# Two attention-fed MLPs on one core: raw weights read in pairs, and the order of the first batch rebuilt

## The chip, the cores and the metric

The kernel runs on one core of one Trainium2 chip. Its time is device microseconds of one launch. Three runs of the kernel before took 931.21, 931.71 and 933.12 us; the median is 931.71 us.

## The reference, cut to what matters

Windowed and global attention over 4 batches and 8 heads, then a gated MLP on normed rows, then a second MLP; everything is float32 in and out.

```python
batch, n_heads, seq_l, seq_g, head_dim = (4, 8, 512, 32, 64)
s_g  = scale * q_g @ k_all.T;   out_g = softmax(s_g) @ v_all        # 32 global queries see everything
s_ll = where(|i - j| <= 32, scale * q_l @ k_l.T, -1e9)              # 512 local queries: a window
s_l  = concat([scale * q_l @ k_g.T, s_ll]);  out_l = softmax(s_l) @ concat([v_g, v_l])
x = concat([out_g, out_l]).transpose(0, 2, 1, 3).reshape(B * S, H * D)   # 4 * 544 = 2176 rows
xn = x / sqrt(mean(x * x) + 1e-6) * rms_g                           # rms_g: 512 gains
y = (silu(xn @ w_gate) * (xn @ w_val)) @ w_out                      # w_gate, w_val: 512 x 1536, w_out: 1536 x 512
h = y @ w_in;  out = maximum(0.01 * h, h) @ w_out2                  # 512 x 2048, 2048 x 512
```

The weights come to the device as 64-bit words (512 KB for a 128 x 512 block) and are narrowed to float32 there.

## The kernel before, in words

**Attention** goes by half units `k` (two query tiles of 128 of one head pair; `half_unit`, L242). A half unit has the steps p (products into PSUM), e (masked maximum on VectorE L263, exp on ScalarE L266), n (norm on VectorE, L278 to L286), t (transposes on TensorE, L302 and L304), c and d (copies of the transposed weights, on ScalarE and VectorE, L311), v (values on TensorE, into `po`) and x (copy of the result to `xl`, L338). The global queries of a head pair are a `global_pair` (L350): G1 scores and their maximum, Gn norm, G2 turned weights, G3 values (`pz_g`), G4 the copies of the result into `x_glob` (L422, L423). `vz` holds the values of the global keys, brought by DMAs that GpSimd issues (L236); `bd` holds the global queries of a batch, block-diagonal.

**The first batch** is written by hand: the string `FIRST` (L484) is read item by item and each item issues its instructions, so every engine gets its own in that order. q, s and g are the first block's norm: squares (L552), their sums (L563) and the multiplication by the gains (`xg`, L570, with the gains in `gcol`); R is the root; a and o narrow one block of weights (`a01`: step 0, block 1); L loads a part of a later unit and Q loads global queries.

**The first MLP** takes its 2176 rows in three blocks of 512 and a tail of 640 in two halves. A block has 12 steps f of 128 hidden columns. A step has three weight blocks k: 0 gate, 1 value, 2 out. In block 0 they come as raw words (`w_0`, `w_1`, ... in the trace, tags w640, w641, w642 with 2, 2 and 1 buffers) by `fetch` (L710), are narrowed by `convert` (L739: one ScalarE instruction `nc` L108, two VectorE instructions `nr` L110 and `wf` L115), stored as float32, split into a high and a low part (`halves_of`, L89 and L92) and multiplied as three products (`mm3`, L85). Steps 0 and 1 use the float32 weights directly (L1005). Block 1 reads the float32 weights back, stores the split form and the sums that the tail needs (`sums_of`); block 2 reads the split form. Beside blocks 0 to 2 the attention of batches 1 to 3 runs, at places given by the table `PLAN`. In block 2 the gaps also take the second MLP's weights (`raw2`, `narrowed`, L874 to L915): 32 jobs of 512 KB, each one load (`w64b`), one narrowing and one store, each load one job ahead.

The first batch, the tail and the second MLP run in the order of the code. Between them the framework's scheduler sets the order of each engine from the code and the pins (`PINS`). A buffer of a pool is filled again only when its last reader is done, and a queue (SP's above all) works in order: a load that waits for a buffer holds up all that stands behind it.

## Time and profile before

| | us |
|---|---|
| runs | 931.21, 931.71, 933.12 (median 931.71) |
| profiled execution | 927.5 |
| its span in the trace | 925.7 |
| TensorE busy in the span | 903.1 (98%) |
| VectorE, ScalarE, GpSimd busy | 616.3, 464.1, 54.4 |
| DMA traffic | 218.05 MB, 236 GB/s on average |

The span runs from the first to the last instruction of the trace; the profiled execution is 1.8 us longer. TensorE is idle for 925.7 - 903.1 = 22.6 us in the span. Timelines have one row for each run of like instructions; a bracket at its end gives the idle time of that engine just before it and what ended it. Where a wait is for several things, the one that came last by the profile is named.

### The profile page before, as it was taken

The numbers are of one execution on the slowest core, as the hardware profiler recorded it, in microseconds if no ns is written. First come the engines' busy times: TensorE is split into PE (matmuls) and PEld (weight loads), VectorE is DVE, ScalarE is ACT, GpSimd is POOL, SyncE is SP. The second block draws the span as 40 slices with busy tenths as digits, with TensorE's granted clock in tenths as the row PEclk, the third lists the DMA queues.
The fourth block names the chain that finished last, engine by engine and source line by source line (L and its number), as shares of the span: only waits on it lengthen the run. The fifth ranks groups of instructions, "written<-read, shape, count | busy, mean of one in ns | idle before, by whom it ended". The sixth has DMA issues, their size and how long they took to land.

```text
span 925.7 us, 14767 instructions
## 1 busy us (share of the span) xinstructions
PE 903.1 (98%) x5172; PEld 737.3 (80%) x5172; DVE 616.3 (67%) x1376; ACT 464.1 (50%) x985; POOL 54.4 (6%) x130
## 2 busy tenths in 40 slices
PE   6889999999999999999999999999999999999998
PEld 5547777777777777877899999888888888888886
DVE  6799977697767886764787776777566344454332
ACT  6977765555554554545634443555544233344321
POOL 6300010100101000000000000000000000000000
PEclk9999999999999999999999999999999999999999
DMA  9898995898889999974477586776433286631122
GB/s 243 275 357 303 311 339 183 265 337 282 296 289 372 373 414 397 347 244 142 151 280 256 185 277 202 265 262 228 148 93 110 72 300 220 215 127 58 46 62 98
DMA packets 91307, 218.05 MB, mean 236 GB/s; under 512 B 13280, under 2 KB 28640, under 8 KB 89184
## 3 DMA queue, kind: packets, MB, share of 16 engines
q1 hardware_dynamic: 88160, 216.05, 67.7%
q0 software_dynamic: 3072, 1.05, 0.5%
q8 instruction: 41, 0.67, 0.3%
q14 instruction: 34, 0.28, 0.1%
HBM read 150.47 MB, written 66.58 MB: 234 GB/s over the span
## 4 chain that ended last, share of the span: by engine, by line
PE 86%; DMA 4%; DVE 2%; ACT 1%; SPq 1%; issue 0%; DVEq 0%
PE o L85 19%; PE pg L85 10%; PE yp L85 10%; PE pv L85 9%; PE px L85 5%; PE pz L85 4%; PE py L85 4%; PE yt L85 4%; PE po L156 3%; PE sc L156 3%; PE pw L85 2%; PE tz L85 2%; PE tx L85 2%; PE ty L85 2%; DMA w64b<-w 2%; PE po L85 1%
## 5 line engine op out<-in xcount | busy, mean ns | idle before, releaser
L85 PE MATMUL o<-wr,d 128*128 128x512 f32 x768 | 174.4, 389 | 0.0
L85 PEld LDWEIGHTS o<-wr,d 128*128 128x128 f32 x768 | 144.1, 188 | 29.9
L85 PE MATMUL pg<-xh,w 128*128 128x512 f32 x272 | 88.9, 408 | 1.0 <-ACT xh L89 1.0
L85 PE MATMUL pv<-xh,w 128*128 128x512 f32 x272 | 86.5, 399 | 0.0
L85 PE MATMUL yp<-hsh,w 128*128 128x512 f32 x288 | 84.8, 399 | 0.9 <-ACT hsh L89 0.9
L266 ACT ACTIVATE s_ring<-s_ring,mx 128x224 f32<-128x224 f32 x128 | 60.6, 478 | 33.2 <-DVE mx L263 33.1
L85 PEld LDWEIGHTS yp<-hsh,w 128*128 128x128 f32 x288 | 53.2, 188 | 14.1 <-issue 1.9
L92 DVE TENSOR_TENSOR d<-h,d 128x512 fp32r<-128x512 f32 x64 | 42.0, 688 | 33.4 <-ACT d L89 33.4
L85 PEld LDWEIGHTS pg<-xh,w 128*128 128x128 f32 x272 | 48.5, 188 | 17.0 <-issue 4.9
L85 PEld LDWEIGHTS pv<-xh,w 128*128 128x128 f32 x272 | 49.6, 188 | 11.6 <-issue 0.5
L89 ACT CAST d<-h 128x512 fp32r<-128x512 f32 x64 | 38.3, 621 | 35.9 <-PE o L85 35.9
L85 PE MATMUL pg<-xl,w 128*128 128x512 f32 x136 | 53.7, 395 | 0.0
L85 PE MATMUL pv<-xl,w 128*128 128x512 f32 x136 | 53.3, 392 | 0.0
L89 ACT CAST w<-wf 128x512 fp32r<-128x512 f32 x68 | 41.5, 618 | 19.9 <-PE pv L85 16.3
L85 PE MATMUL pz<-ysb,wr 128*128 128x512 f32 x192 | 49.1, 391 | 0.0
L85 PE MATMUL yp<-hsl,w 128*128 128x512 f32 x144 | 49.1, 398 | 0.0
L263 DVE CUSTOM_DVE_ANT_0 s_ring<-sc,masks 128x224 f32<-128x224 f32 x128 | 42.9, 389 | 8.5 <-POOL vz L1067 4.9
L236 POOL DMA_DIRECT2D vz<-v_b x64 | 32.0, 503 | 257.5 <-PE po L156 253.5
L92 DVE TENSOR_TENSOR w<-wf,w 128x512 fp32r<-128x512 f32 x68 | 46.4, 689 | 0.7 <-ACT w L89 0.7
L92 DVE TENSOR_TENSOR wr<-wr 128x1024 fp32r<-128x1024 f32 x16 | 19.6, 1225 | 40.3 <-ACT wr L89 40.2
L1302 ACT ACTIVATE h<-h 128x1536 f32<-128x1536 f32 x16 | 23.8, 1490 | 42.8 <-DVE h L954 42.8
L85 PE MATMUL yt<-hst,w 128*128 128x320 f32 x288 | 42.6, 309 | 0.8 <-DMA w<-w_dram 0.8
(227 smaller groups left out, 1790.9 us busy)
## 6 DMA issues: line engine op xcount, KB each, us to landing
w<-w_dram SPq DMA_DIRECT2D x72, 512.0 KB, 5.1
w<-w SPq DMA_DIRECT2D x36, 512.0 KB, 6.3
w_dram<-w SPq DMA_DIRECT2D x36, 512.0 KB, 4.8
w64b<-w SPq DMA_DIRECT2D x32, 512.0 KB, 7.7
w_dram<-wr SPq DMA_DIRECT2D x8, 1792.0 KB, 8.1
wr<-w_dram SPq DMA_DIRECT2D x8, 1792.0 KB, 7.4
kq<-kqv SPq DMA_DIRECT2D x32, 352.0 KB, 6.1
w_f<-wf SPq DMA_DIRECT2D x36, 256.0 KB, 5.2
```

What stands on the lines that cost most here:

```text
L85: nc.tensor.matmul(dst, lhs[a], rhs[b], start=first and i == 0, stop=last and i == 2, skip_group_check=onto)
L89: nc.scalar.copy(hi, src)
L92: nc.vector.tensor_tensor(out=lo, in0=src, in1=hi.bitcast(F32), op=ALU.subtract)
L156: x = nc.tensor.matmul(dst, lhs, rhs, start=start, stop=stop, skip_group_check=bool(onto))
L236: queue.dma_start(out=vz_ring[u % 3][r:r + SG, i, c], in_=v_b[b, p][0:SG, 0, c])
L263: nc.vector.tensor_tensor_reduce(out=sp, in0=sc[j][:, i * KW:(i + 1) * KW], in1=mask_of(t), scale=-scale, scalar=3.0e38, op0=ALU.add, op1= ...
L266: x = nc.scalar.activation(out=sp, in_=sp, func=AF.Exp, bias=mx[:, c:c + 1], scale=-1.0, accum_out=sm[:, c:c + 1])
L1302: nc.scalar.activation(out=out, in_=x, func=AF.Prelu, alpha=0.01)
```

## The change

1. **Gate and value weights of a step go as one.** The raw words of both are one transfer of 1 MB into one tile (tag w64, 2 buffers); they are narrowed one after the other at the place of the value weights; the float32 form is one store and one read of 512 KB (`w_both`). The out weight keeps its own (w642, 1 buffer; `w_last`). The sums for the tail use w642's one buffer in place of w640's two, and are read back as one. Float32 tiles: 2 of double size (wfb) and 3 single (wf), in place of 7 single.
2. **The second MLP's raw weights** come as 16 jobs of 1 MB into the same w64 tiles, in place of 32 jobs of 512 KB.
3. **The first batch is rebuilt.** Masks and `vz` are cleared by VectorE; GpSimd makes the first masks, then `ident`, then issues the first `vz` loads, then makes the last mask. The products of half unit 0 go to four PSUM banks in place of two. The first batch's global queries come by one DMA, and two GpSimd copies put them into `bd`. The gains come as 4 rows of 128 and are turned by TensorE (item c) in place of a DMA of 512 single elements. G01 is cut in G0p (products) and G0e (maximum, exp) with n2 between; `FIRST` has a new order; E0, the load of the exp table, is an item of its own in place of standing right behind the root; a02 and o02 (the out weight of step 0) are now in `FIRST`.

```diff
-            wraw[g, k] = mb.tile([P, DM, 2], U32, tag=f"w64{k}", bufs=W64[k], name=f"w64{k}_{f}")
-            nc.sync.dma_start(out=wraw[g, k], in_=words(w1[f])[:, k])
+            if k:
+                t = mb.tile([P, DM, 2], U32, tag="w642", bufs=1, name=f"w642_{f}")
+                wraw[g, 2] = t
+                nc.sync.dma_start(out=t, in_=words(w1[f])[:, 2])
+            else:
+                t = mb.tile([P, 2, DM, 2], U32, tag="w64", bufs=2, name=f"w64_{f}")
+                wraw[g, 0], wraw[g, 1] = t[:, 0], t[:, 1]
+                wraw[g, "both"] = t.rearrange("p k c t -> p (k c) t")
+                nc.sync.dma_start(out=t, in_=words(w1[f])[:, 0:2])
...
+    def full_tile(g, k):
+        if k:
+            wf[g, 2] = mp.tile([P, DM], F32, tag="wf", bufs=3, name=f"wf2_{g}")
+            return
+        t = wf[g, "both"] = mp.tile([P, 2 * DM], F32, tag="wfb", bufs=2, name=f"wfb_{g}")
+        wf[g, 0], wf[g, 1] = t[:, 0:DM], t[:, DM:2 * DM]
...
+        if k == 0:
+            return
+        full_tile(g, k - 1 if k == 1 else k)
...
+            if k == 1:
+                for x in range(2):
+                    narrow(mb, wf[g, x], wraw[g, x], f"{x}_{f}")
+            else:
+                narrow(mb, wf[g, 2], wraw[g, 2], f"{k}_{f}")
         kept_weights(g, k)
...
-        nc.sync.dma_start(out=w1_f32[step_of(g)[1]][k], in_=wf[g, k])
+        if k == 1:
+            nc.sync.dma_start(out=w1_both[f].rearrange("p k c -> p (k c)"), in_=wf[g, "both"])
+        else:
+            nc.sync.dma_start(out=w1_last[f], in_=wf[g, 2])
         if step_of(g + W64[k])[0] == 0:
-            fetch(g + W64[k], k)
+            fetch(g + W64[k], k - 1 if k == 1 else k)
...
-        ws = mb.tile([P, 4, HK], F32, tag="w640", bufs=W64[0], name=f"ws{f}")
+        ws = mb.tile([P, 4, HK], F32, tag="w642", bufs=1, name=f"ws{f}")
...
-    def narrowed(f, k):
+    def narrowed(f):
         raws = []
         def make():
-            wf = mp.tile([P, DM], F32, tag="wf", bufs=7, name=f"wfb{k}_{f}")
-            narrow(mb, wf, raws[0], f"b{k}_{f}")
-            nc.sync.dma_start(out=w2_f32[f][k], in_=wf)
-        return [lambda: raws.append(raw2(f, k)), make]
+            t = mp.tile([P, 2 * DM], F32, tag="wfb", bufs=2, name=f"wfc_{f}")
+            for k in range(2):
+                narrow(mb, t[:, k * DM:(k + 1) * DM], raws[0][:, k * DM:(k + 1) * DM], f"c{k}_{f}")
+                nc.sync.dma_start(out=w2_f32[f][k], in_=t[:, k * DM:(k + 1) * DM])
+        return [lambda: raws.append(raw2(f)), make]
...
+            qs = qg_t[:, b * NP:(b + 1) * NP, :]
+            if not b:
+                t = mb.tile([P, P], F32, tag="rs", name=f"qs{b}").rearrange("p (n q) -> p n q", q=SG)
+                nc.sync.dma_start(out=t, in_=qs)
+                qs = t
...
+                    nc.gpsimd.tensor_copy(bd[0][r, :, o:o + SG], qs[r])
...
     FIRST = ("p0 e0 p1 e1 "
-             "n0 p2 t0 c0 e2 d0 Q0 "
-             "n1 p3 v0 t1 c1 x0 e3 d1 G01 "
-             "n2 p4 v1 t2 c2 x1 z0 e4 d2 q0 s0 g0 L40 L41 L50 L51 "
+             "n0 p2 t0 c0 e2 d0 "
+             "n1 p3 v0 t1 c1 x0 e3 d1 G0p "
+             "n2 G0e p4 v1 t2 c2 x1 z0 e4 d2 c L40 L41 L50 L51 "
              "n3 p5 v2 t3 c3 x2 e5 d3 G0n G02 "
-             "n4 p6 v3 t4 c4 x3 e6 d4 a00 "
-             "n5 p7 v4 t5 c5 x4 e7 d5 o00 G03 r0 L42 "
-             "n6 v5 t6 c6 x5 q1 g1 n7 d6 G04 t7 "
-             "s1 v6 c7 x6 q2 d7 L52 "
-             "v7 s2 x7 q3 s3 g2 R0 g3 a01 o01 a10 a11 o10 o11")
+             "n4 p6 v3 t4 c4 x3 e6 d4 a00 q0 "
+             "n5 p7 v4 t5 c5 x4 G03 e7 d5 o00 s0 r0 L42 "
+             "n6 v5 t6 n7 c6 d6 t7 v6 c7 x5 d7 q1 v7 s1 x6 q2 s2 x7 L52 Q0 "
+             "q3 s3 g0 R0 g1 a01 g2 o01 g3 a02 a10 o02 E0 a11 o10 G04 o11")
...
-            nc.scalar.activation(out=early_root, in_=eps, func=AF.Exp)
             anchors["recip"] = nc.vector.reciprocal(out=rs[:, 0:m], in_=rs[:, 0:m]).ins
...
-        with nc.allow_non_contiguous_dma(reason="512 gains, one column a chunk"):
-            nc.sync.dma_start(out=gcol, in_=rms_g.rearrange("(c p) -> p c", p=P))
+        nc.sync.dma_start(out=grow, in_=rms_g.rearrange("(c p) -> c p", p=P))
```

How it moves the instructions, at three places. First GpSimd at the start of the kernel: `masks` are the window masks, `bd` the global queries, `vz` the global values that `po` needs. Before:

```order
L188 AFFINE_SELECT masks<-masks 128x32
L191 MEMSET masks 128x32
L196 MEMSET bd_197 64x4x32
L197 MEMSET bd_197 64x4x32
L196 MEMSET bd_198 64x4x32
L197 MEMSET bd_198 64x4x32
L1067 MEMSET vz_190 128x256
L236 DMA vz_190<-v_b 32x64 x4
L1067 MEMSET vz_191 128x256
L236 DMA vz_191<-v_b 32x64 x4
```

After:

```order
L193 AFFINE_SELECT masks<-masks 128x32
L196 AFFINE_SELECT masks<-masks 128x32
masks.py:197 MEMSET ident 128x128
masks.py:199 AFFINE_SELECT ident<-ident 128x128
L244 DMA vz_178<-v_b 32x64 x4
L186 AFFINE_SELECT masks<-masks 128x128
L188 AFFINE_SELECT masks<-masks 128x128
L193 AFFINE_SELECT masks<-masks 128x32
L244 DMA vz_179<-v_b 32x64 x4
L244 DMA vz_180<-v_b 32x64 x4
```

The first four `vz` loads now stand ahead of the last mask and of all of `bd`.

Second ScalarE at the end of the first batch: `pt` are transposed attention weights, `po` attention results on their way to `xl`, `sq` squares of the first block's norm, `xg` the rows times their gains. Before:

```order
L552 ACTIVATE sq_1_721<-xl_409 128x512
L570 ACTIVATE xg<-xl_409,gcol 128x512
L422 COPY x_glob<-px_g_732 64x2x32
L423 COPY x_glob<-px_g_732 64x2x32
L311 COPY pt_7_757<-pp_7_736 128x512
L338 COPY xl_409<-po_744 128x256
L552 ACTIVATE sq_2_760<-xl_409 128x512
L338 COPY xl_409<-po_772 128x256
L552 ACTIVATE sq_3_787<-xl_409 128x512
L570 ACTIVATE xg<-xl_409,gcol 128x512
L594 ACTIVATE rs<-pm_790,eps 128x128
```

After:

```order
L320 COPY pt_6_710<-pp_6_697 128x512
L320 COPY pt_7_734<-pp_7_714 128x512
L347 COPY xl_397<-po_684 128x256
L583 ACTIVATE sq_1_739<-xl_397 128x512
L347 COPY xl_397<-po_721 128x256
L583 ACTIVATE sq_2_756<-xl_397 128x512
L347 COPY xl_397<-po_741 128x256
L583 ACTIVATE sq_3_770<-xl_397 128x512
L601 ACTIVATE xg<-xl_397,gcol 128x512
L625 ACTIVATE rs<-pm_774,eps 128x128
L601 ACTIVATE xg<-xl_397,gcol 128x512
L110 ACTIVATE nc_0_789<-w_0_290 128x512
```

Both copies to `x_glob` and one `xg` left the stretch ahead of the last `pt`, and the multiplications by the gains all stand behind the last square.

Third SP's queue where the second MLP's first raw weights are asked for. `w64b_0` are the raw words of its step 0, half 0 and half 1. Half 1 of steps 0 and 1 is asked for early before, too (beside the first MLP's last raw weights); half 0 waits for a tile of tag w640, which it shares with the sums `ws`, until near the end of the first MLP's second block. Before, there:

```order
L877 DMA w64b_0_3861<-w 128x1024
L768 DMA w_sums_139<-ws_3709 128x1024
L760 DMA w_dram_10_170<-w_22_3591 128x1024
L877 DMA w64b_1_3928<-w 128x1024
L877 DMA w64b_2_4069<-w 128x1024
L877 DMA w64b_2_4040<-w 128x1024
L914 DMA w_fours_100<-wfb_0_3895 128x512
```

After:

```order
L761 DMA w_11_1858<-w 128x2048
L807 DMA w_both_73<-wfb_1846 128x1024
L756 DMA w_10_1915<-w 128x1024
L809 DMA w_last_85<-wf_9_1908 128x512
L935 DMA w64b_3786<-w 128x2048
L807 DMA w_both_74<-wfb_1973 128x1024
L756 DMA w_11_2030<-w 128x1024
L809 DMA w_last_86<-wf_10_2023 128x512
L935 DMA w64b_3844<-w 128x2048
L232 DMA v_1747<-kqv 64x2x512
L233 DMA v_1747<-v_b 32x2x512
L234 DMA v_1747<-kqv 32x2x512
```

Both halves of steps 0 and 1 are now asked for beside the last raw weights of the first MLP (`w_10`, `w_11`), with no `ws` between, since the sums left the raw weights' tag.

## Rows read from the trace of the kernel before

**Rows 1.** The page: its first line and the shares of the chain that ended last.

```profile
span 925.7 us, 14767 instructions
...
PE 86%; DMA 4%; DVE 2%; ACT 1%; SPq 1%; issue 0%; DVEq 0%
```

**Rows 2.** Busy time by stretch: from:to, us, each engine's busy us, PEclk, DMA share, GB/s.

```profile
0.00:70.00 70.00, 55.91 (x481) 37.26 (x481) 56.00 (x195) 55.43 (x157) 25.80 (x69) 1.00 0.97 292
...
200.00:300.00 100.00, 98.33 (x659) 75.99 (x658) 75.01 (x206) 50.63 (x125) 12.17 (x26) 1.00 0.89 316
300.00:500.00 200.00, 200.00 (x1242) 166.55 (x1241) 144.28 (x338) 102.12 (x237) 4.09 (x9) 1.00 0.80 292
```

**Rows 3.** Busy time by stretch, a stretch in which DVE is full.

```profile
50.00:60.00 10.00, 8.74 (x41) 4.23 (x40) 10.00 (x38) 9.73 (x31) 2.14 (x5) 1.00 1.04 405
```

**Rows 4.** Timeline of PE: start us, us, engine, line, work, [idle before, releaser].

```profile
13.23 0.44 PE L156 MATMUL po<-pt,vz 128*64 128x128 f32 x4 [1.07 <-DVE sgl L286]
...
36.83 0.45 PE L156 MATMUL po<-pt,v 128*64 128x64 f32 x8 [1.21 <-ACT pt L311]
...
39.47 3.81 PE L1005 MATMUL pg<-xg,wf 128*128 128x512 f32 x8
...
51.92 0.63 PE L394 MATMUL pg_g<-ident,sg_g 128*128 128x128 f32 x4 [1.26 <-ACT sg_g L375]
...
69.35 0.33 PE L304 MATMUL pp<-ident,sgl 128*128 128x128 f32 x1 [2.13 <-ACT pt L311]
```

**Rows 5.** Timeline of DVE, columns as in rows 4.

```profile
14.94 0.29 DVE L311 COPY pt<-pp 128x128 f32<-128x128 f32 x1 [0.58 <-PE pp L304]
16.11 0.69 DVE L370 TENSOR_REDUCE gm_g<-sa_g 128x1 f32<-128x512 f32 x1 [0.88 <-PE sa_g L156]
...
26.31 0.42 DVE L110 TENSOR_SCALAR nr<-w 128x512 uint32<-128x512 uint32 x1
```

**Rows 6.** Timeline of POOL, a clear and the first unit's global values.

```profile
4.54 0.20 POOL L196 MEMSET bd<- 64x128 f32 x1
...
6.13 2.10 POOL L236 DMA_DIRECT2D vz<-v_b  x4 [0.31 <-POOL vz L1067]
```

**Rows 7.** DMAs issued from 7.6 to 7.9: tile, queue, count, KB each, us to landing.

```profile
vz<-v_b POOLq DMA_DIRECT2D x2, 8.0 KB, 5.9
```

**Rows 8.** Timeline of SP's queue: the raw weights of step 0 and a later half.

```profile
16.89 1.91 SPq L722 DMA_DIRECT2D w<-w  x3
...
43.86 0.38 SPq L722 DMA_DIRECT2D w<-w  x1
```

**Rows 9.** DMAs issued from 16.7 to 17.3, columns as in rows 7.

```profile
w<-w SPq DMA_DIRECT2D x1, 512.0 KB, 8.3
```

**Rows 10.** DMAs issued from 17.7 to 18.1.

```profile
w<-w SPq DMA_DIRECT2D x1, 512.0 KB, 8.8
```

**Rows 11.** DMAs issued from 43.8 to 43.95.

```profile
w<-w SPq DMA_DIRECT2D x1, 512.0 KB, 4.0
```

**Rows 12.** Timeline of ACT, from the first block's norm to its first step.

```profile
35.14 0.72 ACT L570 ACTIVATE xg<-xl,gcol 128x512 f32<-128x512 f32 x1
...
36.20 0.59 ACT L311 COPY pt<-pp 128x512 f32<-128x512 f32 x1
...
40.00 1.28 ACT L596 ACT_TABLE_LOAD   x1
```

**Rows 13.** Waits of ACT from 44 to 110: what waited for what, us, times, longest.

```profile
ACT nc L108 <- DMA w<-w: 4.3, 5, 1.9
```

**Rows 14.** Timeline of SP's queue: the second MLP's first raw weights.

```profile
267.85 0.50 SPq L877 DMA_DIRECT2D w64b<-w  x1
```

**Rows 15.** Timeline of ACT around it.

```profile
274.56 1.24 ACT L108 ACTIVATE nc_b<-w64b 128x512 f32<-128x512 f32 x2 [3.84 <-DMA w64b<-w]
```

**Rows 16.** Timeline of PE around it.

```profile
276.33 0.45 PE L156 MATMUL po<-pt,v 128*64 128x64 f32 x8 [0.78 <-ACT pt L311]
...
288.75 2.11 PE L85 MATMUL yp<-hsh,w 128*128 128x512 f32 x8 [0.89 <-ACT hsh L89]
```

More of the change, by code (lines that the diff above doesn't have):

```diff
@@ L63, in tile_window_global_attention_two_mlps @@
     y_dram = dram.tile([P, KC, NTOK], F32, name="y_dram")
-    w1_f32 = [[dram.tile([P, DM], F32, name=f"w1_f32{k}_{f}") for k in range(3)] for f in range(NF1)]
+    w1_both = [dram.tile([P, 2, DM], F32, name=f"w1_both{f}") for f in range(NF1)]
+    w1_last = [dram.tile([P, DM], F32, name=f"w1_last{f}") for f in range(NF1)]
     HK = KC // 2 * P
@@ L165, in tile_window_global_attention_two_mlps @@
     gcol = const.tile([P, KC], F32, name="gcol")
+    grow = mp.tile([P, 2 * DM], F32, tag="w2", bufs=3, name="grow")[0:KC, 0:P]
     eps = const.tile([P, 1], F32, name="eps")
@@ L355, in scores, with products @@
         def scores():
-            sa, sb = bank("sa" + tg), bank("sb" + tg)
+            products()
+            flush()
+            exps()
+        def products():
+            sa, sb = hold["sab"] = bank("sa" + tg), bank("sb" + tg)
             hold["ve"] = [at.tile([G2, P], F32, tag=f"ve{n}", bufs=1, name=f"ve{n}" + tg) for n in range(2)]
@@ L366, in scores, with exps @@
                       for h in range(2) for n, r, q in both])
-            flush()
+        def exps():
+            sa, sb = hold["sab"]
             g = hold["g"] = at.tile([P, (NT + 1) * P], F32, tag="sg", name="sg" + tg)
@@ L423, in turned_out @@
             later(lambda: nc.scalar.copy(x_glob[D:P, p0:p0 + 2, c:c + SG], v[D:P, :, SG:G2]))
-        return scores, norm, turned, values, turned_out
+        return scores, norm, turned, values, turned_out, products, exps
     def global_queries(b):
         if b < B:
+            qs = qg_t[:, b * NP:(b + 1) * NP, :]
[3 more added lines that the diff above has]
+                qs = t
             for r, o in ((slice(0, D), 0), (slice(D, P), SG)):
-                nc.sync.dma_start(out=bd[b % 2][r, :, o:o + SG], in_=qg_t[r, b * NP:(b + 1) * NP, :])
+                if b:
+                    nc.sync.dma_start(out=bd[b % 2][r, :, o:o + SG], in_=qs[r])
+                else:
+                    nc.gpsimd.tensor_copy(bd[0][r, :, o:o + SG], qs[r])
     def attention(b, unit_done=None):
@@ L501, in first_batch, with gains @@
                 "o": weights, "r": lambda t: nc.scalar.activation(out=early_root, in_=eps, func=AF.Sqrt),
-                "R": spread_later, "z": lambda t: spaced(NP - 1, nc.gpsimd)}
+                "R": spread_later, "E": lambda t: nc.scalar.activation(out=early_root, in_=eps, func=AF.Exp), "z": lambda t: spaced(NP - 1, nc.gpsimd)}
+        def gains(t):
+            pg = bank("gains")
+            nc.tensor.transpose(pg[:, 0:KC], grow, ident[0:KC, 0:KC])
+            nc.vector.tensor_copy(gcol, pg[:, 0:KC])
+        more["c"] = gains
         for t in FIRST.split():
-            (more.get(t[0]) or do)(t)
+            (more.get(t if t == "c" else t[0] if t[0] != "c" else "") or do)(t)
             flush()
@@ L872, in operands, with raw2 @@
         split(t[:, 0, k, :, d:d + w], t[:, 1, k, :, d:d + w], q[:, lo_slot:lo_slot + m])
-    def raw2(f, k):
-        r = mb.tile([P, DM, 2], U32, tag=f"w64{k}", bufs=W64[k], name=f"w64b{k}_{f}")
-        nc.sync.dma_start(out=r, in_=words(w2[f])[:, k])
-        return r
+    def raw2(f):
+        r = mb.tile([P, 2, DM, 2], U32, tag="w64", bufs=2, name=f"w64b_{f}")
+        nc.sync.dma_start(out=r, in_=words(w2[f]))
+        return r.rearrange("p k c t -> p (k c) t")
     def weight_sums(q):
@@ L925, in narrowing @@
     def narrowing():
-        return one_ahead([narrowed(f, k) for f in range(NF2) for k in range(2)])
+        return one_ahead([narrowed(f) for f in range(NF2)])
     def columns_in(s, k, d, q=None):
@@ L1065, in tile_window_global_attention_two_mlps @@
         constants()
-        for u in range(3):
-            nc.gpsimd.memset(vz_ring[u], 0.0)
-            spaced(u, nc.gpsimd)
         global_queries(0)
```

74 lines of the change are left out of this document (43 added, 31 removed).

## The prediction

> **What bounds the kernel now.** I read the page first: TensorE carries 86% of the chain that ended last, out of a span of 925.7 us [rows 1]. So a microsecond counts only where TensorE stands still. The table of stretches says where: 70 - 55.91 = 14.1 us of its idle time lie before 70 us, 1.67 between 200 and 300, and none from 300 to 500 [rows 2]. The rest of the 22.6 us idle is small change, and from 500 us on nothing that the change touches stands in its way. Then I read the timelines. In the opening TensorE waits for whatever finishes last of VectorE, ScalarE and a DMA [rows 4]; from 50 to 60 us VectorE is busy 10.00 of 10 us and the DMA share is over 1, so there those two set the pace and TensorE's idle time is only their shadow [rows 3]. The change therefore has three places to gain or lose: before the first raw weight is needed (to 26 us), the norm of the first block (34 to 46 us), and the start of the second MLP's narrowing (268 to 289 us).
>
> **Place 1, to 26 us.** TensorE waits 1.07 us at 13.23 [rows 4]. The row names VectorE's `sgl`, but the other input of these products is `vz`, whose four loads GpSimd issues from 6.13 for 2.10 us [rows 6], and a load issued near 7.7 takes 5.9 us [rows 7], so the last lands near 13.6. In the new order these loads pass four clears of `bd`, 0.20 us each [rows 6], VectorE takes the 0.31 us clear of `vz` [rows 6], and the last mask is passed too: 0.80 + 0.31 = 1.11 us and more, so the wait of 1.07 ends. What follows is late by it: VectorE waits 0.58 us for the transposes and 0.88 for the global products [rows 5]. The second of these is also covered by the cut of G01, since n2 now stands between products and maximum. So VectorE should come 0.58 + 0.88 = 1.46 us earlier to the next steps, TensorE with it.
>
> This lead meets the first raw weights. VectorE's first narrowing instruction ran at 26.31, without waiting [rows 5]. The gate half was issued at 16.89 [rows 8] and took 8.3 us [rows 9], so it was there at 25.2. The value half took 8.8 us [rows 10] from the second third of that issue row, 16.89 + 2 x 0.64 - 0.25 = 17.9: there at 26.7. One transfer of both is there when both are: between 25.2 and 26.7. One issue of some 0.5 us fewer stands ahead of it on SP's queue, so I take 26.2, near the upper end. VectorE, 1.46 us ahead, would come at 24.85 and wait 1.35 us in front of it, with the exps and norms of the later half units queued behind it. Of the lead 0.1 us is left. At 25.2 it would be 1.1, at 26.7 minus 0.4: that is the bound from both sides of this edit.
>
> The rest of place 1 I cost at nothing. The clears that VectorE takes over lie ahead of its first exp, where it is idle. The transpose and copy of the gains (128 x 4) are one small instruction each, no longer than the 128 x 128 copy of 0.29 us [rows 5]. The two GpSimd copies into `bd` are not in the trace; a copy of 64 x 128 elements should cost between nothing and the 0.5 us of a GpSimd issue [rows 6] (2.10 / 4), each; I take 0.25, and they are hidden as long as `bd` is there at some 13.8, when the products of G0p can begin. If not, VectorE still has n2 to do before it needs them. The Trainium skill ("SBUF — State Buffer", section "Who interferes with whom") says that GpSimd and a VectorE instruction on the shared ports shut each other out for a whole instruction. By that rule each copy could wait for one VectorE instruction, 0.69 us by the longest here [rows 5], and G0p would be late by up to 1.4 us, which n2 would cover mostly; no row here shows such a pair.
>
> **Place 2, the norm of block 1.** ScalarE's order between its row at 35.14 and the last `pt` at 36.20 holds one `xg` and two copies to `x_glob` [rows 12]: 1.06 us, and TensorE waited 1.21 us for that `pt` [rows 4]. All three leave the stretch. What follows on ScalarE (copy, square, copy, square) is the chain to the root and moves up with it. In return all four `xg` stand behind the last square; one of about 0.7 us [rows 12] must be done before `pg` can begin, where before it was not in the way. Against that the exp table's load, 1.28 us [rows 12], no longer stands behind the root, and so the other `xg` are there when TensorE asks for the next chunk (3.81 us for four chunks, 0.95 each [rows 4], against 0.72 for one `xg` [rows 12], with one narrowing between). I put the start of `pg` at 38.5 with a bound of 38.1 in place of 39.47, and the end of the stretch between 0.5 and 1.1 us earlier. With the 0.1 us kept from place 1 the first step comes 0.9 us earlier. Bounds: 2.0 with place 1's lead kept, and -1.0 where the third edit below bites.
>
> That edit is the raw weights of step 2. Before, the value half alone was asked for late, at 43.86 [rows 8], and was there 4.0 us later [rows 11]. Now gate and value are asked for together, after both halves of step 0 are narrowed, which I put at 41 to 42 (four ScalarE instructions of some 0.7 us behind 38.5). With no queue in front 1 MB takes the 4.0 us and about 1.2 more for its second half (a queued 512 KB takes 512 KB / 405 GB/s = 1.3 us by the full stretch [rows 3]), so it is there at 46.2 to 47.2, against 47.9 for the late half before. ScalarE comes to it at about 46 and waits some 0.5 us; the tanh and the exps of the next unit are queued behind it. So I keep the 0.9 us through the stretch to 76 us, in which VectorE's work (the same instructions as before) sets the pace. In the middle ScalarE waits five times, 4.3 us in all, for raw words [rows 13]. Merging removes some of these and makes others longer; I take no change. The Trainium skill ("DMA: Bandwidth & Descriptors", section "Anatomy of one DMA") has a fixed part of about 2 us a transfer beside its bytes, so that a pair would save 2 us; the trace has three raw transfers asked for within 1.91 us [rows 8], and the first two of them take 8.3 and 8.8 us [rows 9, 10], so there any fixed part lies beside other transfers; where a pair is waited for by itself the forecast would gain up to 2 us by the rule.
>
> **Place 3, 268 to 289 us.** The first of the second MLP's raw loads is asked for at 267.85 [rows 14], and ScalarE waits 3.84 us for it until 274.56 [rows 15], with a `pt` and a `w` behind it. TensorE pays 0.78 us at 276.33 and 0.89 at 288.75 [rows 16], which together are the whole 1.67 us of [rows 2]. Now the first pairs are asked for beside `w_10` and `w_11`, at the end of the first MLP's first block, and have long landed. I count the 1.67 us as gained. What is late next: a pair gives ScalarE two narrowings in a row (1.24 us for two [rows 15]), and the one buffer of `ws` can hold up SP. From 300 to 500 TensorE has no idle time, so its supply there has slack. I charge 0.1 us, with a bound of 0.9 (the price of one such wait of TensorE [rows 16]).
>
> **Sum.** -0.9 (places 1 and 2) - 1.67 + 0.1 = -2.5 us. The profiled execution took 927.5 us, 1.8 over its span, and the median of the runs is 931.7, 4.2 over it; I take the difference to the median: 931.7 - 2.5 = **929.2 us**.
>
> **Rivals.** A: the lead is not lost at the first raw weight. For it: the row at 26.31 did not wait, and the transfer could land at 25.2; the whole of the opening's idle time is 14 us. Then 1.1 to 1.46 us stay, place 2 gives its 1.1, and the wait of 2.13 us at 69.35 [rows 4], which is VectorE's and ScalarE's lateness, shrinks by some 0.8: -1.67 - 1.4 - 1.1 - 0.8 = -5.0, 926.7 us; with the 1.26 us at 51.92 [rows 4] gone as well 925.4. Against it: the arithmetic of the two halves above.
>
> B: no change. The lead of place 2 is spent when the value half, which was there early, is replaced by a pair that is asked for later; and the wait at 268 us is replaced by others of the same size, since the narrowing has the same work and the scheduler spaces it by its own estimates. 930.5 to 931.7, I write 931 us.
>
> C: slower. From 44 to 110 us ScalarE works in order and narrows raw words among the exps. A pair can only begin when its last byte is there and its tile comes free only when both halves are narrowed, so each of the five waits [rows 13] can grow by the 1.3 us of a half's passage: 6.5 us. Place 1 and 2 then give nothing, place 3 its 1.67 and half of the waits' shadow is hidden or not: all of it shown on TensorE gives 931.7 + 6.5 - 1.67 = 936.5, and with the 0.9 of places 1 and 2 kept 935.6. It decides from the point at which the five waits grow by more than 2.5 us together. For it: VectorE and the DMAs are full from 50 to 60 us [rows 3], so nothing that is lost there can be made good. Against it: fewer issues on SP and as many bytes.
>
> **How the numbers follow.** Forecast 0.40 (its own range 927.6 to 930.8: bounds of place 1 and 2, and 0.9 for place 3's new wait), A 0.20, B 0.20, C 0.20. Changes under 0.2%, 1.9 us, can't be told from none in this kernel's runs, so faster begins below 929.8. Of the forecast two thirds lie there, and all of A: 0.27 + 0.20 = 0.47. Same is the rest of the forecast, all of B and a fifth of C, 0.13 + 0.20 + 0.04 = 0.37. Slower is the rest of C, 0.16. The range runs from A's far end, 925.4, to 935.2, where C is half in.
>
> **What would show it.** Right: no wait of TensorE at its first `po<-pt,vz`; VectorE's first `nr` preceded by a wait of about 1.3 us for `w_0`; `pg` at about 38.5; no wait on `w64b` near 274 us and TensorE's busy time of 200 to 300 at 99 or more. Wrong: `nr` at 25 us without a wait (A); ScalarE's waits for raw words from 44 to 110 us at 8 us or more (C); TensorE's idle time before 70 us still at 14 us and a new wait behind 250 us (B).

## The result, and the profile after

The changed kernel is slower: median 941.79 us (940.89 to 944.27, 4 runs) against 931.46 us (929.45 to 933.12, 4 runs), a ratio of 1.0118 with a 95% interval of 1.0101 to 1.0135. The forecast was 929.2 us. The profiled execution took 944.27 us, its span 942.5. It is the longest of the four, and that of the kernel before (927.5) is among the shortest of its kernel (927.08 to 937.51 us over all comparisons), so of the 16.8 us between the two traces only 10.3 lie between the medians.

The page: its first line, the busy times and the chain's shares.

```profile
span 942.5 us, 14629 instructions
...
PE 916.4 (97%) x5173; PEld 743.9 (79%) x5173; DVE 618.1 (66%) x1384; ACT 464.2 (49%) x985; POOL 53.2 (6%) x126
...
PE 88%; DMA 4%; ACT 3%; DVE 2%; issue 1%; SPq 1%; ACTq 0%; DVEq 0%
```

The span grew by 16.8 us [rows 1]. TensorE does the same matmuls, yet it is busy for 916.4 - 903.1 = 13.3 us more and idle for 26.1 - 22.6 = 3.5 us more. VectorE and ScalarE are busy as long as before. The same matmuls took longer because the clock was lower: the mean granted clock of this execution is 0.987 against 0.997, which over the span makes, as an estimate, (0.013 x 942.5) - (0.003 x 925.7) = 9.5 us of full-speed time; the rest of the 13.3 us I did not take apart. The stretches that answer to [rows 2], and those in which the clock fell (columns as there, PEclk is the third from the end):

```profile
0.00:70.00 70.00, 57.66 (x463) 38.17 (x464) 55.99 (x199) 53.34 (x153) 24.46 (x65) 0.93 0.89 272
200.00:300.00 100.00, 97.19 (x606) 74.35 (x605) 77.20 (x224) 52.26 (x133) 8.05 (x17) 0.98 0.81 287
300.00:500.00 200.00, 199.43 (x1233) 162.00 (x1232) 139.09 (x334) 101.24 (x236) 8.16 (x18) 1.00 0.81 294
```

```profile
50.00:55.00 5.00, 1.76 (x11) 1.41 (x8) 5.00 (x18) 3.58 (x15) 0.00 (x0) 0.80 1.06 404
55.00:60.00 5.00, 5.00 (x9) 2.06 (x8) 4.72 (x18) 4.71 (x15) 0.00 (x0) 0.52 0.97 356
115.00:120.00 5.00, 3.16 (x16) 2.45 (x16) 4.97 (x12) 3.95 (x11) 0.00 (x0) 0.79 0.99 326
135.00:140.00 5.00, 5.00 (x33) 3.39 (x32) 4.35 (x12) 2.84 (x7) 0.80 (x3) 0.50 1.05 352
280.00:285.00 5.00, 5.00 (x31) 3.81 (x30) 4.07 (x16) 2.85 (x10) 1.99 (x4) 0.67 0.92 284
```

A clock of 0.50 is 1.2 GHz, the lower of the two levels. Each of these stretches holds or follows waits of TensorE, so these waits were paid for once as idle time and again as slow matmuls beside or behind them.

**Where the time went.** Every step of the first MLP has one tanh on ScalarE, so the starts of the 36 tanhs are a common ruler. The first of the changed kernel, the sixth, the seventh, the thirteenth (the first of block 1), the nineteenth, the twentieth and the last:

```profile
48.96 0.62 ACT L1087 ACTIVATE th<-gate 128x512 f32<-128x512 f32 x1
...
108.04 0.57 ACT L1087 ACTIVATE th<-pg 128x512 f32<-128x512 f32 x1
...
131.42 0.58 ACT L1087 ACTIVATE th<-pg 128x512 f32<-128x512 f32 x1
...
206.72 0.58 ACT L1087 ACTIVATE th<-pg 128x512 f32<-128x512 f32 x1
...
270.11 0.60 ACT L1087 ACTIVATE th<-pg 128x512 f32<-128x512 f32 x1 [0.83 <-PE pg L86]
...
286.23 0.60 ACT L1087 ACTIVATE th<-pg 128x512 f32<-128x512 f32 x1 [1.48 <-PE pg L86]
...
461.89 0.60 ACT L1087 ACTIVATE th<-pg 128x512 f32<-128x512 f32 x1 [0.94 <-PE pg L86]
```

The same seven in the kernel before:

```profile
48.52 0.62 ACT L1028 ACTIVATE th<-gate 128x512 f32<-128x512 f32 x1
...
105.47 0.60 ACT L1028 ACTIVATE th<-pg 128x512 f32<-128x512 f32 x1
...
121.23 0.57 ACT L1028 ACTIVATE th<-pg 128x512 f32<-128x512 f32 x1
...
195.60 0.60 ACT L1028 ACTIVATE th<-pg 128x512 f32<-128x512 f32 x1
...
259.36 0.58 ACT L1028 ACTIVATE th<-pg 128x512 f32<-128x512 f32 x1
...
269.62 0.60 ACT L1028 ACTIVATE th<-pg 128x512 f32<-128x512 f32 x1
...
445.88 0.60 ACT L1028 ACTIVATE th<-pg 128x512 f32<-128x512 f32 x1 [0.94 <-PE pg L85]
```

So the lag is 0.4 us at the first step, 2.6 at the sixth, 10.2 at the seventh, 11.1 at the end of block 0, 10.8 at the nineteenth, 16.6 at the twentieth and 16.0 at the last. The loss has two places: in block 0 mainly the step from 108 to 131 us, and later the one step from 270 to 286 us.

**Block 0.** ScalarE, VectorE, SP's queue, the DMAs of that queue and TensorE around 120 us:

```profile
118.23 0.72 ACT L110 ACTIVATE nc<-w 128x512 f32<-128x512 f32 x1
124.30 1.23 ACT L110 ACTIVATE nc<-w 128x512 f32<-128x512 f32 x2 [5.35 <-DMA w<-w]
...
124.24 0.76 DVE L112 TENSOR_SCALAR nr<-w 128x512 uint32<-128x512 uint32 x2 [3.87 <-DMA w<-w]
```

```profile
112.41 0.37 SPq L761 DMA_DIRECT2D w<-w  x1
...
115.03 0.33 SPq L756 DMA_DIRECT2D w<-w  x1
```

```profile
w<-w SPq DMA_DIRECT2D x1, 1024.0 KB, 9.3
...
w<-w SPq DMA_DIRECT2D x1, 512.0 KB, 9.2
```

```profile
115.70 0.45 PE L158 MATMUL po<-pt,v 128*64 128x64 f32 x8 [1.41 <-ACT pt L320]
117.30 3.33 PE L86 MATMUL yp<-hsh,w 128*128 128x512 f32 x8 [1.14 <-ACT hsh L90]
```

What ScalarE and VectorE wait for is the raw out weight of a step (the load of L756). Its tile has one buffer, so it was asked for at 115.03, right behind its last reader (an `nr` that began at 114.54), and then it stood behind a pair of 1 MB issued at 112.41, which landed at 121.7: it landed itself at 115.03 + 9.2 = 124.2. Both engines work in order, and nothing behind the narrowing ran for 3.9 us on VectorE and 5.4 on ScalarE.

**The step from 270 to 286 us.** VectorE, SP's queue and TensorE:

```profile
277.56 0.76 DVE L834 TENSOR_TENSOR ws<-wfb 128x256 f32<-128x256 f32 x2 [5.52 <-DMA wfb<-w_both]
```

```profile
266.83 0.61 SPq L232 DMA_DIRECT2D v<-kqv  x1
...
270.95 0.42 SPq L234 DMA_DIRECT2D v<-kqv  x1
271.42 0.42 SPq L767 DMA_DIRECT2D wfb<-w_both  x1
```

```profile
279.76 1.02 PE L158 MATMUL sc<-kq 64*128 64x224 f32 x6 [2.81 <-DVE th L1092]
```

VectorE waits for the read-back of a step's float32 gate and value, one transfer now. It was issued at 271.42 behind six value transfers of the attention. The products of gate and value (`th`) stand behind the sums on VectorE, and TensorE waits 2.81 us for them. In the kernel before VectorE waits near there too, 3.06 us for a single read-back just behind the twentieth tanh, but TensorE waits only 0.78 us there, for a `pt` [rows 16]:

```profile
271.40 0.42 DVE L774 TENSOR_TENSOR ws<-wf 128x256 f32<-128x256 f32 x1 [3.06 <-DMA wf<-w_f]
```

### The profile page after: what moved, and what is told of

Same layout as the page of the kernel before. It is cut to its first block, busy times and chain, and to the rows that moved or that the text cites. A ratio compares the mean times of both kernels' runs of the same rounds, so it can differ in the third digit from the quotient of the medians.

```text
span 942.5 us, 14629 instructions
## 1 busy us (share of the span) xinstructions
PE 916.4 (97%) x5173; PEld 743.9 (79%) x5173; DVE 618.1 (66%) x1384; ACT 464.2 (49%) x985; POOL 53.2 (6%) x126
## 4 chain that ended last, share of the span: by engine, by line
PE 88%; DMA 4%; ACT 3%; DVE 2%; issue 1%; SPq 1%; ACTq 0%; DVEq 0%
PE o L86 18%; PE pg L86 10%; PE yp L86 10%; PE pv L86 9%; PE px L86 4%; PE py L86 4%; PE pz L86 4%; PE sc L158 3%; PE po L158 3%; PE yt L86 3%; PE pw L86 2%; PE tz L86 2%; PE tx L86 2%; PE ty L86 2%; DMA w<-w 2%; DMA w<-w_dram 1%
## 5 line engine op out<-in xcount | busy, mean ns | idle before, releaser
L86 PE MATMUL pg<-xh,w 128*128 128x512 f32 x272 | 90.8, 416 | 0.4 <-ACT xh L90 0.4
L86 PEld LDWEIGHTS yp<-hsh,w 128*128 128x128 f32 x288 | 53.9, 190 | 14.4 <-issue 2.1
L158 PE MATMUL sc<-kq 64*128 64x224 f32 x256 | 43.3, 410 | 7.1 <-DMA kq<-kqv 3.9
L86 PEld LDWEIGHTS yt<-hst,w 128*128 128x128 f32 x288 | 42.3, 188 | 1.7 <-ACT hst L90 1.2
```

The costliest lines, as they stand in the source:

```text
L86: nc.tensor.matmul(dst, lhs[a], rhs[b], start=first and i == 0, stop=last and i == 2, skip_group_check=onto)
L158: x = nc.tensor.matmul(dst, lhs, rhs, start=start, stop=stop, skip_group_check=bool(onto))
```

## The experiments

Times are medians; the ratio is that of the comparison with the kernel before, with its interval. "Lag" is the start of a tanh against the kernel before, in the profiled execution: at the end of block 0 (thirteenth tanh), gained or lost in the step of 270 us (nineteenth to twentieth), and at the last step. A lag is one execution against one execution, and some us of it need no edit: before_ws642 runs the order of the kernel before on every queue up to 120 us, and its sixth tanh (107 us) is 1.6 us late. v_later runs the order of the changed kernel through all of block 0 and ends it at 9.9 in place of 11.1. The kernel before is itself represented by an execution 4 us under its median, so the last column is too high by about that.

| kernel | us | ratio, interval | end of block 0 | step of 270 | last |
|---|---|---|---|---|---|
| changed | 941.79 | 1.0118 (1.0101 to 1.0135) | 11.1 | +5.9 | 16.0 |
| first_only | 934.91 | 1.0048 (1.0029 to 1.0067) | 7.0 | -1.5 | 7.1 |
| pairs_only | 939.97 | 1.0106 (1.0070 to 1.0141) | 6.3 | +7.1 | 12.6 |
| raw_apart | 939.56 | 1.0107 (1.0074 to 1.0141) | 7.3 | +7.1 | 15.4 |
| f32_apart | 941.58 | 1.0115 (1.0088 to 1.0143) | 13.4 | -1.8 | 15.3 |
| before_noraw | 932.04 | 0.9997 (0.9983 to 1.0011) | 2.6 | -0.3 | 3.2 |
| after_noraw | 934.41 | 1.0038 (1.0019 to 1.0057) | -2.3 | +1.7 | 3.5 |
| wfb_three | 941.13 | 1.0091 (1.0063 to 1.0118) | 7.9 | +3.3 | 14.5 |
| read_halves | 942.87 | 1.0119 (1.0097 to 1.0142) | 9.4 | +4.1 | 12.6 |
| v_later | 942.47 | 1.0124 (1.0101 to 1.0147) | 9.9 | +1.0 | 14.4 |
| before_ws642 | 932.44 | 1.0015 (0.9999 to 1.0032) | 4.9 | -0.7 | 6.4 |
| first_consts | 933.67 | 1.0028 (1.0006 to 1.0049) | 3.0 | -1.8 | 4.8 |
| first_order | 935.59 | 1.0055 (1.0035 to 1.0075) | 7.3 | -2.1 | 7.7 |
| out_two | 934.01 | 1.0035 (1.0018 to 1.0052) | 1.7 | +2.4 | 4.2 |
| raw_halves | 939.15 | 1.0098 (1.0074 to 1.0122) | 5.2 | +5.8 | 11.1 |
| before_out_two | 932.01 | 1.0000 (0.9979 to 1.0021) | 3.4 | +3.0 | 5.3 |
| combo_later | 930.16 | 0.9992 (0.9972 to 1.0011) | -2.2 | +0.8 | 3.9 |
| combo_apart | 928.20 | 0.9963 (0.9951 to 0.9976) | -1.3 | +2.3 | -0.9 |

**The change in two parts, and the pairs in two.** first_only is the kernel before with the whole third part of the change; pairs_only is the changed kernel with that part taken back.

> Before with the first batch rebuilt alone; all weights move in halves as before. Theory 1 (the pairs cost the time, because a pair is asked for only when both halves of an earlier one are used up): 928 to 933 us, near the kernel before, and no wait of ScalarE over 3 us for raw words from 100 to 145 us. Rival (the rebuilt first batch costs it, by the lowered clock before 70 us and what follows from it): 938 us or more.

> The changed kernel with the first batch of before; the transfers go in pairs. Theory 1: 939 to 944 us, with the two losses of the changed kernel (some 8 us from 105 to 145 us, some 6 from 268 to 290). Rival (the first batch): 930 to 934 us.

Neither alone: the rebuilt batch costs 3.5 us and the pairs 8.5 by the medians, and the expectation for first_only was missed (934.91 us, and a wait of 3.9 us for raw words); that for pairs_only was met in time. In block 0 they cost 7.0 and 6.3 us and together 11.1; single executions that differ by some us don't tell that from a sum. The step of 270 us belongs to the pairs.

raw_apart, in `fetch` (`...` marks lines left out, here and below):

```diff
-                t = mb.tile([P, 2, DM, 2], U32, tag="w64", bufs=2, name=f"w64_{f}")
...
-                nc.sync.dma_start(out=t, in_=words(w1[f])[:, 0:2])
+            wraw[g, k] = mb.tile([P, DM, 2], U32, tag=f"w64{k}", bufs=W64[k], name=f"w64{k}_{f}")
+            nc.sync.dma_start(out=wraw[g, k], in_=words(w1[f])[:, k])
```

> The changed kernel with the raw words in halves again, both MLPs (each half asked for and narrowed at its own place); only the float32 form of gate and value still goes and comes as one. Theory 1: the loss from 105 to 145 us goes (ScalarE waits under 3 us there for raw words), that from 268 to 290 us stays: 933 to 938 us. Rival (the pairs as such do no harm, what hurts is the order that the scheduler happens to give after any edit): no pattern, anywhere from 930 to 945 us.

f32_apart, in `full_tile`, and each store and read by itself:

```diff
...
-        t = wf[g, "both"] = mp.tile([P, 2 * DM], F32, tag="wfb", bufs=2, name=f"wfb_{g}")
...
+        wf[g, k] = mp.tile([P, DM], F32, tag="wf", bufs=7, name=f"wf{k}_{g}")
```

> The changed kernel with the float32 form in halves again (seven single tiles, a store and a read for each block); the raw words still come in pairs, both MLPs. Theory 1: the loss from 105 to 145 us stays, VectorE's wait of 5.5 us for the read-back near 277 us goes: 935 to 940 us. Rival as for raw_apart.

Their times missed: both stay near the changed kernel. Their step of 270 us came out as expected: +7.1 with the float32 pair kept, -1.8 without it. So the double read-back is part of that loss: it is there in pairs_only and raw_apart, gone in first_only and f32_apart, and of all kernels with single read-backs none loses more than 3.0 us in that step. It is not enough by itself: after_noraw and out_two below keep it, behind the same six transfers on SP's queue, and lose 1.7 and 2.4. And no gain in time from taking it away alone is shown, since f32_apart stays at 941.58 us. The first block did not come out as expected: it keeps 7.3 us of loss without raw pairs.

**Is it the raw words at all?** In both kernels, loads of raw words of the first MLP are left out once each tile has been filled, and the old words are narrowed again. The edit in the kernel before (in the changed kernel a pair's two halves go together):

```diff
+        if i == 0 and g >= W64[k]:
+            wraw[g, k] = wraw[g - W64[k], k]
...
```

> The kernel before without the raw loads of the first MLP from step 2 on (out weights from step 1 on): the words of an earlier step that still lie in the tile are narrowed again. Everything else is done. With after_noraw it asks whether waits for raw words make the loss of the first block. Theory 2 (waits for raw words idle VectorE and ScalarE in the first block, where they set the pace, and the clock falls with TensorE's waits): 922 to 931 us, at most a few us faster than with the loads, since it waits little there.

> The changed kernel without the same raw loads. Theory 2: the loss of the first block (11 us at its last step against the kernel before) goes and the loss at the read-back (6 us near 280 us) stays, so that it is 5 to 8 us slower than before_noraw. Rival (the order of the instructions itself costs the first block its time, not the raw words): it stays 10 us or more slower than before_noraw.

Without these loads the changed kernel ends block 0 2.3 us ahead of the kernel before and 4.9 ahead of its own partner, in place of 11.1 behind. So the order of the first batch and the pairs lose nothing there by themselves: the loss is waiting for raw words. From there to the last step it still loses 5.8 us, but not where that was expected: 1.7 in the step of 270 us and 3.3 behind it. The difference of the two medians, 2.4 us, is smaller than expected, because block 0 became a gain. before_noraw missed its range too, at 932.04 us.

**The read-back: tile, size or queue?** wfb_three: `wfb` with three buffers, `wf` with one. read_halves: two transfers into the same tile. v_later: the plan of the third batch's attention puts both value loads (`L42`, `L52`) at step 11.

```diff
-                nc.sync.dma_start(out=wf[g, "both"], in_=w1_both[f].rearrange("p k c -> p (k c)"))
+                for x in range(2):
+                    nc.sync.dma_start(out=wf[g, x], in_=w1_both[f][:, x])
```

```diff
...
+    LATE = dict(PLAN)
+    LATE.update({5: "0:G02;2:T4+N5;4:G03;5:V4+L40 S6", 7: "2:T6+N7;5:V6", 11: "0:L42;3:L52"})
```

> The changed kernel with three float32 tiles of double size and one single in place of two and three: the same memory, one more step of look-ahead for the read-back of gate and value. Theory 3 (at 270 to 290 us VectorE waits because a pair's tile comes free only when both halves are used up, so the load is asked for late): that loss of some 6 us goes, unless the single tile of the out weight makes one of its own; 934 to 938 us. Rival (a 512 KB read lands later than two of 256 KB): the loss stays, 940 us or more.

> The changed kernel in which the float32 gate and value of a step are read back as two transfers of 256 KB into the halves of the same tile, with the same number of tiles. Theory 3: the loss at 270 to 290 us stays, 940 to 944 us. Rival (size of the transfer): it goes, 934 to 937 us.

> The changed kernel in which two value loads of the third batch (six transfers on SP's queue) are asked for two to six steps later in the second block, behind the read-back of the float32 gate and value of the block's eleventh step. Theory 4 (the read-back is late because it stands behind these six on the queue, and as one transfer it carries both halves): VectorE's wait of 5.5 us near 277 us goes, 936 to 939 us. Rival (the time of the read-back is set by its tile or by its size): the wait stays, 940 to 944 us.

Two transfers in place of one change little (+4.1), and the third tile takes away only part (+3.3); neither is shown to be the cause, and wfb_three's time missed its range. With the read-back ahead of the six transfers the step costs +1.0. It was issued 5.9 us earlier (265.52), and VectorE's longest wait there fell from 5.5 us to 2.6. First row v_later, second the changed kernel, from 262 to 282 us:

```profile
DVE ws L837 <- DMA wfb<-w_both: 2.6, 1, 2.6
```

```profile
DVE ws L834 <- DMA wfb<-w_both: 5.5, 1, 5.5
```

So the place on the queue moves the pair's coming. It is not the only thing that does: with the queue's order kept, out_two's wait there is 3.6 us and after_noraw's 2.9. And the time did not fall: 942.47 us, an outright miss. In block 2 VectorE now waits, for the store of a narrowed pair that still holds one of the two double tiles (first row, 300 to 350 us), and TensorE for VectorE behind it:

```profile
DVE wfc L117 <- DMA w_f<-wfc: 6.0, 2, 4.0
```

```profile
341.08 0.73 PE L86 MATMUL pg<-xh,w 128*128 128x512 f32 x2 [1.66 <-DVE th L1091]
```

In the changed kernel that wait is 1.4 us. From the twentieth tanh to the last v_later loses 3.9 us where the changed kernel gains 0.6: the gain was given back one block later, at the same tiles.

**The edits in the first batch, and the one gain of place 3.** first_consts has the new clears, masks, loads of `vz`, queries and gains; first_order has the new `FIRST`; before_ws642 moves the sums to the tag w642 and nothing else.

```diff
-        ws = mb.tile([P, 4, HK], F32, tag="w640", bufs=W64[0], name=f"ws{f}")
+        ws = mb.tile([P, 4, HK], F32, tag="w642", bufs=W64[2], name=f"ws{f}")
```

> The kernel before with the new clears, masks, global loads, global queries and gains, but the order of the first batch as before (the turn of the gains put in at the same place as in the changed kernel). The opening's waits for the global values go. Theory 2 (a lead in the opening is worth nothing while the raw words set the pace behind it): 929.5 to 932 us. Rival (these edits make the loss of first_only): 934 us or more.

> The kernel before with the new order of the first batch alone (clears, masks, queries and gains as before). Theory 2: it carries most of first_only's 3.5 us, with TensorE's wait behind the root table's load near 32 us and a late exp of the next global pair near 53 us: 933 to 937 us. Rival: 930 to 932 us.

> The kernel before with one edit: the tail's sums use the out weight's raw tile, so that the second MLP's first half 0 is asked for as early as half 1. It is the gain of 1.67 us that the prediction put at 268 to 289 us, alone. Theory of the prediction: the waits there go, 929.0 to 930.5 us. Rival (the scheduler gives another order and with it other waits of the same size): 930.5 to 934 us.

The new order carries first_only's loss, as expected (7.3 us in block 0, against 7.0). The new clears and loads gain nothing: level to 0.0 us at the second tanh, then 3.0 behind at the end of block 0, with a time between the two expected ranges. before_ws642 gains nothing either: its waits for `w64b` near 274 us are gone, and TensorE waits 1.35 and 1.32 us for `pt` near 294 instead. The 3.0 and 4.9 us in block 0 of first_consts and before_ws642 can't be put down to their edits, since 1.6 us of the 4.9 arose while the order was still that of the kernel before. The intervals of the three reach from no loss to 0.75%.

first_only and first_order lose most of their lag in one step: 1.9 us at the second tanh and 5.9 at the third, 2.7 and 6.7. There ScalarE waits for raw words, longer than anywhere in block 0 of the kernel before (1.9 us at most), and TensorE waits for a `pt` behind it. From first_only:

```profile
73.57 0.68 ACT L108 ACTIVATE nc<-w 128x512 f32<-128x512 f32 x1 [3.91 <-DMA w<-w]
...
75.42 0.39 PE L311 MATMUL pp<-ident,sgl 128*128 128x128 f32 x1 [3.29 <-ACT pt L318]
```

In first_order the two waits are 3.43 and 4.21 us, and the granted clock from 75 to 80 us is 0.66 and 0.50 in the two.

**Depth of the out weight's raw tile, and size of the raw pair.** out_two is the changed kernel with two buffers for w642 and one for `wf` in place of three, the same memory; raw_halves issues a raw pair as two transfers, and before_out_two is the kernel before with two buffers for w642 and five for `wf`.

```diff
-                t = mb.tile([P, DM, 2], U32, tag="w642", bufs=1, name=f"w642_{f}")
+                t = mb.tile([P, DM, 2], U32, tag="w642", bufs=2, name=f"w642_{f}")
...
-            wf[g, 2] = mp.tile([P, DM], F32, tag="wf", bufs=3, name=f"wf2_{g}")
+            wf[g, 2] = mp.tile([P, DM], F32, tag="wf", bufs=1, name=f"wf2_{g}")
...
-    W64 = (2, 2, 1)
+    W64 = (2, 2, 2)
...
```

> The changed kernel with two raw tiles for the out weight in place of one (the float32 tiles of the out weight go from three to one, the same memory). Theory 5 (in the first block the out weight's raw words come last, behind a pair of 1 MB, and with one tile they can't be asked for earlier; ScalarE's and VectorE's waits of 5.4 and 3.9 us near 124 us are for them): the loss of the first block falls from 11 us to 6 us or less at its last step, and the wait near 124 us goes. Rival (the pairs themselves are late): it stays at 8 us or more.

> The changed kernel in which the raw words of gate and value are asked for together, as now, into the same tile, but as two transfers of 512 KB each. Theory 5 (what counts is when a pair may be asked for, not its size): the loss of the first block stays at 8 to 13 us. Rival (a transfer of 1 MB lands later than its first half needs): it falls to 7 us, as without pairs.

> The kernel before with two raw tiles for the out weight and five float32 tiles in place of seven. If the depth of the out weight's raw tile sets the first block's pace also before: 926 to 930 us, faster than both kernels. If not: 930 to 934 us.

out_two takes back 7.8 of the 10.3 us, and both its expectations were met. Block 0 ends 1.7 us behind in place of 11.1. ScalarE's waits for raw words from 44 to 150 us, first the changed kernel, then out_two (us, times, longest):

```profile
ACT nc L110 <- DMA w<-w: 13.2, 7, 5.3
```

```profile
ACT nc L110 <- DMA w<-w: 1.5, 1, 1.5
```

With less waiting the granted clock was higher, too: from 100 to 150 us first the changed kernel, then out_two.

```profile
100.00:150.00 50.00, 45.11 (x266) 32.50 (x266) 38.62 (x102) 30.31 (x79) 4.29 (x9) 0.90 0.96 331
```

```profile
100.00:150.00 50.00, 48.89 (x334) 37.99 (x332) 44.65 (x122) 36.64 (x93) 6.37 (x13) 1.00 0.88 310
```

That the one `wf` buffer isn't what helped is seen in wfb_three, which has it too and ends block 0 7.9 us behind. raw_halves ends block 0 5.2 us behind, below the 8 to 13 that were expected, but that is not the wait: the order of all four engines that compute is that of the changed kernel through block 0, ScalarE still waits 4.5 us for the out weight, and from the sixth tanh to the seventh it goes from 0.9 us ahead to 7.4 behind, 8.3 us against the changed kernel's 7.6. The rest of the difference lies elsewhere, and the intervals of the two times overlap, so the size of a raw pair is not shown to count. The kernel before gains nothing from a second tile, although its waits for raw words go: 8.4 us in 8, none over 1.9, become one of 0.9. So the sum of such waits is not the measure: many short ones cost nothing in that kernel, and one long one costs 7.6 us in this one.

**Together.** combo_later joins out_two, raw_halves and v_later; combo_apart joins out_two, raw_halves and f32_apart (with five `wf` buffers).

> The changed kernel with the three edits that each took a loss away: two raw tiles for the out weight, a raw pair asked for together but as two transfers, and the six value transfers of the third batch behind the read-back. If the losses are separate: first block within 2 us of the kernel before, the read-back's loss of 6 us gone, 926 to 932 us. If each gain is given back at the next coarse buffer (VectorE waits for the narrowed pair's store in the third block, as it did with v_later): 932 to 936 us.

> The changed kernel with two raw tiles for the out weight, raw pairs as two transfers, and the float32 form of all weights in single tiles and halves again (five tiles). The rebuilt first batch and the early request of the second MLP's pairs stay. If the double float32 tiles make what was left of out_two's 3.3 us: 928 to 932 us. If not: 933 to 937 us.

Both times came out in the better of the two expected ranges. combo_apart is faster than both kernels: 928.20 us, 0.37% under the kernel before with an interval of 0.24 to 0.49%. Its page and TensorE's stretches (those of the first part above):

```profile
span 925.0 us, 14747 instructions
...
PE 903.2 (98%) x5173; PEld 736.3 (80%) x5173; DVE 618.5 (67%) x1384; ACT 464.3 (50%) x985; POOL 53.1 (6%) x126
```

```profile
0.00:70.00 70.00, 55.39 (x474) 36.48 (x474) 57.87 (x203) 54.95 (x156) 24.42 (x65) 1.00 0.99 301
200.00:300.00 100.00, 99.39 (x660) 76.42 (x659) 73.83 (x201) 48.84 (x123) 12.13 (x26) 1.00 0.86 306
```

TensorE is busy 903.2 us again, and from 200 to 300 us it has 0.6 us of idle time in place of 1.67 [rows 2]. By the tanhs that is no gain yet: 1.3 us ahead at the end of block 0, 0.9 ahead at the last step. combo_later reached the expected time but not a difference from the kernel before.

## Why the prediction was wrong

- **Place 1, the wait at 13.23: right.** TensorE's first `po<-pt,vz` begins at 11.98 without a wait, against 13.23 [rows 4].
- **Place 1, the lead lost at the first raw weight: wrong.** VectorE's first narrowing instruction does not wait and starts 1.40 us earlier than at 26.31 [rows 5]:

```profile
24.91 0.43 DVE L112 TENSOR_SCALAR nr<-w 128x512 uint32<-128x512 uint32 x1
```

  SP issued the raw load of both halves at 15.15, not at 16.89 [rows 8]; I had counted one issue fewer and not the waits ahead of it on the queue. That was rival A's condition, and its time did not follow.
- **Place 2: right for `pg`, wrong for the step.** `pg` starts at 38.69 (I had 38.5). The raw words of step 2 were asked for at 41.53 (I had 41 to 42) and took 6.2 us, not 5.2, so ScalarE waited 1.66 us, not 0.5, and the first tanh was 0.4 us late, not 0.9 early. A wait that I had not named is new, too: the root's table load now stands ahead of both last `pt`, and TensorE waits 1.71 us, with the clock at 0.75 from 30 to 35 us. In the other kernels with the new order (first_only, after_noraw, out_two) TensorE waits 1.7 us there as well. And the wait of 1.26 us at 51.92 [rows 4] became one of 3.24. Over the first 70 us TensorE is idle 12.3 us in place of 14.1, at a clock of 0.93 in place of 1.00.

```profile
32.76 1.08 PE L311 MATMUL pp<-ident,s_ring 128*128 128x128 f32 x4 [1.71 <-ACT early_root L527]
...
53.93 1.08 PE L410 MATMUL pg_g<-ident,sg_g 128*128 128x128 f32 x4 [3.24 <-ACT sg_g L391]
```

- **The middle, "I take no change": the step that failed.** This term of 0 measured 11.1 - 0.4 = 10.7 us in the trace (7.8 by the medians, if out_two's second tile is taken as the measure). I had read the waits for raw words from 44 to 110 us [rows 13], and there they stayed as they were: 4.8 us in 4 against 4.3 in 5. The loss came right behind, from 108 to 131 us, with the one wait of 5.35 us for the out weight; from 44 to 150 us ScalarE waits 13.2 us against 8.4. For the rest of block 0 the term of 0 had no reason given. Rival C named the mechanism (in-order narrowing, a tile that comes free late) at 0.20. Its sign, 8 us or more from 44 to 110 us, did not show; it looked at the pairs, where the out weight behind a pair was the one waited for, and priced no clock.
- **Place 3: the waits went, the gain did not come.** No engine waits for `w64b` near 274 us. But in the same stretch stands the read-back's loss of 5.9 us, and TensorE's busy time from 200 to 300 us is 97.19, not 99 or more. I had not priced that edit at all, since I had looked at the requests that become earlier and not at those that become later. The 0.1 us for what is late next was charged for two narrowings in a row and for the one buffer of `ws`.
- **The size of a transfer.** The Trainium skill ("DMA: Bandwidth & Descriptors", section "Measured (HBM→SBUF, 128 partitions, SWDGE, issued from GpSimd)") advises batching transfers to 1 MiB or more. Its figures, like those of the section on a transfer's fixed part that the prediction named, are for loads that GpSimd issues; the raw loads here are issued by SP. For the bandwidth of one stream no run here speaks against it. Here, with the DMA share at 0.96 from 100 to 150 us, what counted was when a load could be asked for and what it stood behind: raw_halves, the same bytes in the same tiles as two transfers, lost 8.3 us in the step where the changed kernel lost 7.6.

What stays open: the new order of the first batch alone costs 3.5 us by the medians. Its traces put the loss at one wait of 3.4 to 3.9 us for raw words near 74 us, and without raw loads the loss is gone with that order and the pairs together; but the order alone without raw loads was not tried, so this is read and not shown. Nor was it tried which of combo_apart's three edits are needed, or why f32_apart is no faster without the double read-back.

## What to carry to other kernels

Before merging two loads, write down for each buffer when its last reader is done, since that is when the next load can be asked for. A merged load is asked for at the later of the two times, can be used only when all of it has landed, and what is asked for behind it comes later: here the out weight landed 2.5 us behind a pair, 9.2 us after it was asked for. Where engines work in order and have no slack, look at the shallowest tile of the ring, not at the merged one: one more buffer there, for the same memory elsewhere, gave back 7.8 of 10.3 us. And a gain won at one such place can be given back at the next coarse tile (v_later). Before a lag between two traces is put down to an edit, look at how far two executions with the same order of instructions lie apart.

## What the runs showed of the hardware that was not expected

A wait of TensorE could be paid for more than once. In the changed kernel waits of 1.41 and 1.14 us near 116 us, and of 2.81 us at 279.76, each stand beside a stretch with a granted clock of 0.79 and 0.67; over the whole execution the lower clock makes 9.5 us of full-speed time by the estimate above, and the added idle time is only 3.5 us. The clock was 1.00 over 100 to 150 us in out_two, where TensorE ran 334 matmuls with 1.1 us of idle time, in place of 266 with 4.9. Not every wait was followed by a lower clock: in out_two the wait of 1.71 us near 35 us stands in a stretch, 30 to 40 us, with a clock of 1.00.

Asking for fewer bytes did not make the kernel before faster: before_noraw leaves out most of block 0's raw loads and is at a ratio of 0.9997 (0.9983 to 1.0011). Nor did taking its waits for raw words away with a second tile, at 1.0000 (0.9979 to 1.0021).
